# Nyström attention with a squared-ReLU MLP: the landmark sums of batches 4 to 7 go to GpSimd, and the plan around them is laid out anew

## The chip, the core and the metric

The kernel runs on one core of a Trainium2 chip. The metric is device time in microseconds (us) of one execution; a time is the median of several executions. The engines have their own instruction queues, each run in order: PE (TensorE matmul), ACT (ScalarE), DVE (VectorE), POOL (GpSimd) and SP (SyncE, which here only issues the stores). The loads are issued from POOL's queue, between POOL's computing instructions.

## The reference, cut to what matters

```python
def _attn_ref(q, k, v):                      # 8 batches, 8 heads, 576 rows, 64 columns, fp32
    q_lm = q.reshape(B, H, 32, 18, D).mean(axis=3)     # 32 landmarks, each a mean of 18 rows
    k_lm = k.reshape(B, H, 32, 18, D).mean(axis=3)
    A, Bm, C = sm(q, k_lm), sm(q_lm, k_lm), sm(q_lm, k)   # softmax(scale * a @ b^T)
    Z = Bm^T / (norm1(Bm) * norminf(Bm) + 1e-06)
    for _ in range(6):
        Z = 2 * Z - Z @ Bm @ Z
    return A @ Z @ C @ v

def _moe_ref(x, w_in, w_out):                # x: 4608 tokens x 512, d_ff = 2048
    r = np.maximum(x @ w_in, 0.0)
    return (r * r) @ w_out
```

## The kernel before, in words

Each of the 8 batches has an attention part and an MLP part. Nothing of the attention's result is written out: (Z C v) is multiplied into `w_in` first, which gives a matrix WP per batch, and the MLP's first matmul takes A (transposed) against WP.

**The operations and their names.** The program makes a list of small operations, named by kind, batch and part. For batch b, with the profile's line of each:

- loads on POOL's queue, cast to bf16 on the way: `ldk`, `ldq` (L462), `ldv` (L471), `win` (L481), `wout` (L492). X has 3 buffers, LM 2.
- `lm` sums the 18 rows of every landmark, as matmuls against an identity on PE. Batches 0 and 1 (`FLAT_LM`) take 18 matmuls of 128x128 for each half of the heads (L521, 128 columns each). Batches 2 to 7 take 36 matmuls on 64x64 quarters of the array with 256 columns (L532), which leave two partial sums in two banks: `lmc` (ACT, L552, two copies) brings one to SBUF as LS, `lme` (DVE, L555) adds the other. In batches 0 and 1 `lme` is a plain copy on ACT (L449). `lmt` transposes the result (DVE, L561).
- `T` transposes q and k by blocks (DVE, L506, four a batch).
- `B`, `Bmx` ... `Brn`, `Yi`, `Zi`: the small softmax and the start of the iteration. `N` and `U`: the six steps (PE L666 or L671, DVE L680), with `bd` (L620) which spreads an operand to a block diagonal on POOL or DVE; `Zm` (L759) does it at the end.
- `SC`, `Cmx`, `Cex`, `CT`: the softmax of C and its transpose (PE L697, DVE L708, ACT L714, DVE L719). `Crc` takes the reciprocal of C's row sums, after putting them in the order of the next matmul's output: one copy of 128x2 (L726), four of 32x1 (L729), a reciprocal (L731), all on DVE. `CV` (PE L740, 72 matmuls), `CVe` (DVE L749), `ZC` (PE L766), `ZCe` (L449), `W` (PE L786, 8 matmuls each), `We` (L449 on ACT or L453 on DVE, 128x1024).
- `SA`, `At`, `Amx`, `Asb`, `Aex`, `Asu`, `Arc`, `Aml`, `Ab`: the softmax of A in two parts of 10 and 8 of the 18 segments (PE L808; DVE L833, L836, L840; ACT L842; DVE L844, L847, L850, L853).
- `F` (PE L879): A against WP, 16 pieces of hidden columns a batch, in batches 0 and 1 two parts (320 and 256 columns), so 32 pieces. `R` (ReLU, ACT L896 or DVE L898) and `Q` (square, ACT L905 or DVE L907) bring each piece to G in SBUF. A piece holds one of 4 banks kept for F until its R is done (two banks, when it has 576 columns).
- `O` (PE L925): four groups of four matmuls of 512 columns for each of the 36 output tiles; `Oe` copies out, `St` stores.
- `fill` (L1036): matmuls on ones without use, which fill PE's gaps at the start.

**What sets the order.** A planner (`Plan.schedule`) runs the list against costs that are written in the program (`v_`, `ap_`, `a_`, `g_`, `pe`), chooses an engine where an operation allows several, and gives banks of PSUM. Where several operations are ready, the one with the longest chain behind it (`tail`) goes first; `URGE` shifts this by kind and batch, and `PATIENCE` holds an operation back from one engine in favour of another. An operation with `port` waits, in the plan, until the port of POOL and DVE is free. The instructions are then issued to each engine in the plan's order. On the chip only data, banks and buffers hold an instruction back, and each engine keeps its order.

In the order of before, PE reaches the first `F` with `W0.0 W0.1 fill F0.0`, and then runs F and O pieces with the attention of later batches between them. `F1.0`, the first MLP piece of batch 1, comes behind 14 groups of O; in the changed program it comes behind 10.

Of the kernel before, what the change touches and what calls it, by code (L numbers as in the profile page):

```python
# [8 lines left out]
P = 128  # L9
AF = mybir.ActivationFunctionType  # L10
ALU = mybir.AluOpType
AX = mybir.AxisListType
BF16 = mybir.dt.bfloat16
F32 = mybir.dt.float32
# [5 lines left out]
D = 64  # L20
M = 32
SEG = S // M
# [30 lines left out]
class Plan:  # L53
# [2 lines left out]
    SW_LANES = 8  # L56


    BLOCK, FETCH, FETCH_LOADED, PROLOG = 256, 3.8, 6.2, 80

    SWITCH = 0.092

# [2 lines left out]

    def op(self, name, engs, emit, R=(), W=(), alloc=(), nbytes=0, queue=None, after=(), bias=0.0,
           crit=False, port=(), mode="full", ni=8):
        o = Op()
        o.crit, o.port, o.mode, o.ni = crit, port, mode, ni
        o.name, o.engs, o.emit = name, engs, emit  # L70
        o.deps, o.succ, o.tail, o.seq = set(), [], 0.0, len(self.ops)
        o.alloc, o.nbytes, o.queue, o.bias = list(alloc), nbytes, queue, bias
        o.eng = o.start = o.end = None
        o.uses = [x for x in {id(x): x for x in [*R, *W] if isinstance(x, Bank)}.values()]
        for x in o.uses:
            x.users += 1
        for x in R:
            if x in self.last_w:
                o.deps.add(self.last_w[x])
        for x in W:  # L80
            if x in self.last_w:
                o.deps.add(self.last_w[x])
            o.deps.update(self.readers.get(x, ()))
        for x in R:
            self.readers.setdefault(x, []).append(o)
        for x in W:
            self.last_w[x] = o
            self.readers[x] = []
        o.deps.update(after)
        o.deps.discard(o)  # L90
        self.ops.append(o)
        return o
# [183 lines left out]
    def fillers(self, until, width, emit):  # L276

        busy = sorted((o.start, o.start + o.engs["PE"] + 0.1) for o in self.ops if o.eng == "PE")
        found, at = [], 1.5
        for a, b in busy:  # L280
            if a > until:
                break
            n = min(int((a - 0.2 - at) / width), 8 if at < 6 else 2)
            if n > 0:
                for j in range(8):
                    if all(h[1] >= a or h[2] <= at - 0.1 for h in self.history if h[0] == j):
                        found.append((a - 0.2 - n * width, j, n))
                        break
            at = max(at, b)
        for at, j, n in found:  # L290
            o = Op()
            o.name, o.eng, o.start, o.seq = f"fill{at:.0f}", "PE", at, -1
            o.engs, o.end, o.tail, o.mode = {"PE": n * width}, at + n * width, 0.0, "full"
            o.emit = lambda e, j=j, n=n: emit(j, n)
            self.ops.append(o)
# [11 lines left out]
def ap_(n):  # L307
    return 0.046 + 0.00083 * n


def v_(n, fast=False):
    return 0.07 + (0.00052 if fast else 0.00104) * n


def g_(n):
    return 0.15 + 0.0022 * n
# [28 lines left out]
def pe(n, k=1):  # L345
    return k * max(n * 0.000424, 0.027)
# [3 lines left out]
def kernel(  # L350
# [9 lines left out]
    nc = tc.nc  # L360
# [3 lines left out]
    def mk(name, shape, dt):  # L364
        return sb.tile(shape, dt, name=name, tag=name)
# [3 lines left out]
    def bank(x, i=0):  # L369
        return ps[:, x.at + i, :]  # L370
# [4 lines left out]
    def pair(x, n):  # L375
        return ps[:, x.at:x.at + 2, 0:n]
# [2 lines left out]
    V = [mk(f"V{i}", [P, 2, SEG, D], BF16) for i in range(3)]  # L379
    TT = [mk(f"TT{i}", [P, 2, 2, SEG, M, 2], BF16) for i in range(2)]  # L380
    LM = [mk(f"LM{i}", [P, 2, 2, D], BF16) for i in range(2)]
    LS = [mk(f"LS{i}", [P, 256], F32) for i in range(2)]
    LT = [mk(f"LT{i}", [P, 2, 2, M, 2], BF16) for i in range(2)]
    SAt = [mk(f"SA{u}", [P, 2, n, M], F32) for u, n in enumerate(A_LEN)]
    Anorm = [mk(f"An{u}", [P, 2, n // 2, M, 2], BF16) for u, n in enumerate(A_LEN)]
# [24 lines left out]
    ident = mk("ident", [P, P], BF16)  # L410
# [6 lines left out]
    op = pl.op  # L417
# [8 lines left out]
       R=["identf"], W=["ident"])  # L426
# [10 lines left out]
    def c_blk(e):  # L437
# [3 lines left out]
       R=["onesf"], W=["warm"])  # L441
# [4 lines left out]
    def copy(e, o, i, scale=None):  # L446
        if e == "ACT":
            if scale is None:
                nc.scalar.copy(o, i)  # L449
            else:  # L450
                nc.scalar.activation(o, i, AF.Copy, scale=scale)
        elif scale is None:
            eng(e).tensor_copy(o, i)  # L453
        else:
            eng(e).tensor_scalar(out=o, in0=i, scalar1=scale, scalar2=None, op0=ALU.mult)
# [40 lines left out]
    def attention(b):  # L496
        x, tt, lm, lt = X[b % 3], TT[b % 2], LM[b % 2], LT[b % 2]
        kx = lambda t, r: ("X", b % 3, t, r)
        kt = lambda t, r: ("TT", b % 2, t, r)
        i2 = b % 2  # L500
        quad = lambda i: slice(32 * i, 32 * i + 32)
# [8 lines left out]

        flat = b in FLAT_LM
        rss = ((0,), (1,)) if b in SPLIT_LM else ((0, 1),)
        pls = [Bank(1, "att") for _ in rss] if flat else [Bank(2, "att")]
        pl_ = pls[0]

        def lmx(e, rs):
            if flat:
                for s in range(SEG):  # L520
                    nc.tensor.matmul(  # L521
                        bank(pls[rs[0]])[:, 0:128 * len(rs)].rearrange("p (t x) -> p t x", t=2)
                        .rearrange("p t (r d) -> p t r d", d=D),
                        lhsT=ident[:], rhs=x[:, :, rs[0]:rs[-1] + 1, s, :],
                        start=(s == 0), stop=(s == SEG - 1))
                return
            o = pair(pl_, 256).rearrange("p j (t r d) -> p j t r d", t=2, r=2)
            for s in range(9):
                for j in range(2):
                    for h in range(2):  # L530
                        i, z = slice(64 * h, 64 * h + 64), 64 * (h ^ j)
                        nc.tensor.matmul(o[z:z + 64, j], lhsT=ident[i, i],  # L532
                                         rhs=x[i, :, :, 9 * j + s, :],
                                         start=(s == 0), stop=(s == 8))

        for rs in rss:
            op(f"lm{b}.{rs[0]}", {"PE": pe(128 * len(rs), 18 if flat else 9) + 0.03},
               lambda e, rs=rs: lmx(e, rs), R=["ident", *[kx(t, r) for t in range(2) for r in rs]],
               W=[pls[rs[0]]], alloc=[pls[rs[0]]],
               mode="full" if flat else "64x64", ni=36 if flat else 72)  # L540
        if flat:
            for rs in rss:
                op(f"lme{b}.{rs[0]}", {"ACT": ap_(128 * len(rs)), "DVE": v_(128 * len(rs))},
                   lambda e, rs=rs: copy(
                       e, lm[:, :, rs[0]:rs[-1] + 1],
                       bank(pls[rs[0]])[:, 0:128 * len(rs)].rearrange("p (t r d) -> p t r d",
                                                                      t=2, d=D)),
                   R=[pls[rs[0]]], W=[("LM", i2, r) for r in rs])
        else:
            def lmc(e):  # L550
                for h in range(2):
                    nc.scalar.copy(LS[i2][64 * h:64 * h + 64],  # L552
                                   bank(pl_, 1)[64 - 64 * h:128 - 64 * h, 0:256])
            op(f"lmc{b}", {"ACT": 0.77}, lmc, R=[pl_], W=[("LS", i2)])
            op(f"lme{b}", {"DVE": v_(256)}, lambda e: nc.vector.tensor_tensor(  # L555
                lm[:].rearrange("p t r d -> p (t r d)"), bank(pl_)[:, 0:256], LS[i2][:], ALU.add),
               R=[pl_, ("LS", i2)], W=[("LM", i2, 0), ("LM", i2, 1)])
        kLT = lambda r: ("LT", i2, r)
        for rs in rss:
            sl = slice(rs[0], rs[-1] + 1)  # L560
# [162 lines left out]


        def crc(e):
            nc.vector.tensor_copy(s_[:, 16:18], s_[:, 14:16])  # L726
            for p in range(4):
                z = 2 * (p // 2) + 1 - p % 2
                nc.vector.tensor_copy(s_[quad(z), 16 + p % 2:17 + p % 2],  # L729
                                      s_[quad(p), 15 - p % 2:16 - p % 2])  # L730
            nc.vector.reciprocal(s_[:, 16:18], s_[:, 16:18])  # L731
        op(f"Crc{b}", {"DVE": 0.45}, crc, R=[kb("csm0"), kb("csm1")], W=[kb("crc")])
        pV = Bank(2, "att")


# [313 lines left out]
        "Bnm", "Bad", "Brn", "BBT", "Zi", "Yi", "N", "U", "ZC", "ZCe", "W", "We"}  # L1049
CRIT_B = (0,)  # L1050
SQ_ACT = tuple(range(B))
SPLIT_LM = (0,1)
SPLIT_A = (0,)
FLAT_LM = (0,1)
SA_LATE = (0,)
W_CH = 1

PATIENCE = {"DVE": 0.4}

STRETCH = (1.2, 2.5)  # L1060

URGE = {
    "Aml0": 17, "Aml2": -18, "Amx0": -26.9, "Asb1": -13.2, "At0": 4.5, "BBT2": -20.7,
    "BBT6": -17, "Blo2": -5.9, "Bmb0": 1.6, "CT0": -10.2, "CV3": -4.9, "CVe0": 66.5,
    "Cex1": 35.8, "F0": -27.3, "N1": 27.6, "N3": 46.9, "O0": 29.4, "O1": -1.9, "Q0": 22.2,
    "R0": 162.5, "R1": 8.2, "SA1": 67.9, "SA2": 61.8, "T1": -15.2, "We0": 60.5, "Yi0": 23.4,
    "Zi1": -21.7, "lm1": -67.5, "lm2": -65.6, "lmc3": 11.7
}
POOL_A = ()
POOL_M = ()  # L1070

PARTS = (0,1)
WEAVE = {0: 0.0, 1: 0.5}
LIMITS = {"att": 6, "h": 4, "o": 4}

# [33 lines left out]
```

## Time and profile before

| What | us |
|---|---|
| median of 3 runs (272.32 to 272.54) | 272.36 |
| the profiled execution, whole | 273.66 |
| the profiled execution, span from first to last instruction | 272.0 |
| PE busy in the span | 256.7 |
| ACT busy | 209.4 |
| DVE busy | 180.5 |
| POOL busy | 50.5 |

The span is that of the profiled execution; 1.7 us lie around it. The instructions of one engine overlap a little: their rows give the time from start to end of each, and the next may start some 0.1 us ahead of the end of one that it doesn't depend on. A matmul's row of 0.38 us for 512 columns contains the time until its result has landed; in a stream, matmuls of 512 columns start every 0.215 us. So sums over an engine's queue are made from start to start. The granted TensorE clock is 1.00 throughout.

### The profile page before, as it was taken

How to read it: one execution, taken by the hardware profiler on the slowest of the kernel's cores; microseconds unless marked ns; L12 is line 12 of the kernel's file. 1: busy time of each engine (PE TensorE's matmuls, PEld its weight loads, DVE VectorE, ACT ScalarE, POOL GpSimd, SP SyncE). 2: the span in 40 equal slices, each digit the busy share in tenths (PEclk: the TensorE clock that was granted, in tenths of full speed). 3: DMA queues.
4: the chain of work that ended last, by engine and by line, in shares of the span. 5: the costliest groups of instructions: out<-in, count | busy, mean ns of one | idle time of the engine just before them, and what ended most of it. 6: DMA issues, size and time to landing. Idle time of an engine off the chain costs nothing.

```text
span 272.0 us, 7590 instructions
## 1 busy us (share of the span) xinstructions
PE 256.7 (94%) x3070; PEld 143.8 (53%) x3070; DVE 180.5 (66%) x533; ACT 209.4 (77%) x422; POOL 50.5 (19%) x93
## 2 busy tenths in 40 slices
PE   5868899999999999999999999999999999999993
PEld 1636355455565666465545564555546564555452
DVE  2489999878999789849952898249864898000000
ACT  2033898899999979998799799998829989999110
POOL 8443823634240022000400010000000000000000
PEclk9999999999999999999999999999999999999999
DMA  6999999999996192611542101221031110311333
GB/s 104 202 210 209 204 204 212 232 220 214 242 226 129 41 156 64 126 39 41 85 83 61 46 14 40 58 62 39 4 80 39 41 42 0 80 39 39 80 77 77
DMA packets 16259, 28.28 MB, mean 104 GB/s; under 512 B 2272, under 2 KB 4576, under 8 KB 16224
## 3 DMA queue, kind: packets, MB, share of 16 engines
q0 software_dynamic: 10304, 18.35, 37.5%
q1 hardware_dynamic: 5840, 9.38, 14.0%
q8 instruction: 24, 0.39, 0.6%
q14 instruction: 11, 0.09, 0.1%
q10 hardware_dynamic: 80, 0.07, 0.1%
HBM read 36.70 MB, written 9.44 MB: 170 GB/s over the span
## 4 chain that ended last, share of the span: by engine, by line
PE 51%; DVE 22%; ACT 18%; issue 6%; DMA 2%; POOL 1%; ACTq 0%; DVEq 0%; POOLq 0%
PE ps L925 28%; PE ps L879 13%; ACT RS L896 6%; ACT G L905 5%; ACT WP L449 3%; DVE TT L506 2%; DVE SA L833 2%; PE ps L786 2%; PE ps L532 2%; DMA X<-in_q_dram 2%; DVE G L907 2%; PE ps L697 2%; DVE CT L719 1%; PE ps L521 1%; DVE sm L729 1%
## 5 line engine op out<-in xcount | busy, mean ns | idle before, releaser
L925 PE MATMUL ps<-w_out,G 128*128 128x512 bf16 (+1 forms) x592 | 141.1, 373 | 0.3 <-DVE ST L680 0.3
L896 ACT ACTIVATE RS<-ps 128x576 bf16<-128x576 f32 (+2 forms) x152 | 79.5, 562 | 8.1 <-PE ps L879 5.9
L879 PE MATMUL ps<-AT,WP 128*128 128x288 bf16 (+2 forms) x512 | 80.4, 286 | 1.4 <-ACT WP L449 0.6
L925 PEld LDWEIGHTS <-G 128*128 128x128 bf16 x592 | 55.1, 98 | 49.8 <-issue 4.5
L905 ACT ACTIVATE G<-RS 128x576 bf16<-128x576 bf16 (+2 forms) x119 | 66.3, 590 | 1.5
L879 PEld LDWEIGHTS <-WP 128*128 128x128 bf16 x512 | 46.6, 97 | 28.8 <-issue 7.0
L449 ACT COPY OS<-ps 128x512 f32<-128x512 f32 (+2 forms) x34 | 19.1, 569 | 17.8 <-PE ps L925 17.8
L907 DVE TENSOR_TENSOR G<-RS 128x576 bf16<-128x576 bf16 (+2 forms) x41 | 16.3, 406 | 20.2 <-ACT RS L896 19.9
L449 ACT CAST WP<-ps 128x1024 bf16<-128x1024 f32 x27 | 26.7, 1025 | 3.3 <-PE ps L786 3.3
L506 DVE STREAM_TRANSPOSE TT<-X 128x576 uint32<-128x576 uint32 x32 | 24.0, 758 | 4.9 <-DMA X<-in_k_dram 4.4
L620 POOL TENSOR_TENSOR BD<-ST,blkb 128x256 bf16<-128x256 bf16 x10 | 6.7, 667 | 106.0 <-DVE ST L680 56.4
L708 DVE TENSOR_REDUCE sm<-ps 128x1 f32<-128x576 f32 x16 | 11.5, 750 | 10.4 <-PE ps L697 10.4
L714 ACT ACTIVATE C<-ps,sm 128x576 bf16<-128x576 f32 x16 | 14.1, 906 | 5.5 <-DVE sm L711 5.5
L680 DVE SCALAR_TENSOR_TENSOR ST<-ST,ps 128x128 bf16<-128x128 bf16 (+1 forms) x48 | 12.6, 261 | 7.2 <-PE ps L666 6.7
L453 DVE COPY OS<-ps 128x512 f32<-128x512 f32 (+1 forms) x4 | 2.3, 579 | 22.4 <-ACT OS L449 22.4
L471 POOL DMA_DIRECT2D V<-in_v_dram x24 | 12.7, 538 | 7.6 <-DMA w_in<-in_moe_w_in_dram 2.2
L833 DVE STREAM_TRANSPOSE SA<-ps 128x320 f32<-128x320 f32 (+1 forms) x32 | 12.8, 449 | 1.4 <-ACT RS L896 0.9
L786 PE MATMUL ps<-w_in,ZC 64*32 64x512 bf16 x256 | 12.1, 383 | 1.3 <-ACT ZC L449 0.7
L462 POOL DMA_DIRECT2D X<-in_k_dram x16 | 9.0, 564 | 20.6 <-PE ps L532 14.3
L842 ACT ACTIVATE SA<-SA 128x640 f32<-128x640 f32 (+1 forms) x16 | 10.2, 680 | 3.2 <-DVE SA L840 3.2
L844 DVE TENSOR_REDUCE smA<-SA 128x20 f32<-128x640 f32 (+1 forms) x16 | 11.7, 744 | 1.0 <-ACT SA L842 0.9
L850 DVE TENSOR_TENSOR An<-SA,smA 128x640 bf16<-128x640 f32 (+1 forms) x16 | 12.2, 790 | 0.0
(81 smaller groups left out, 253.2 us busy)
## 6 DMA issues: line engine op xcount, KB each, us to landing
out_dram<-OS SPq DMA_DIRECT2D x70, 128.0 KB, 2.4
X<-in_k_dram POOLq DMA_DIRECT2D x16, 288.0 KB, 10.4
X<-in_q_dram POOLq DMA_DIRECT2D x16, 288.0 KB, 9.7
V<-in_v_dram POOLq DMA_DIRECT2D x8, 288.0 KB, 9.2
w_in<-in_moe_w_in_dram POOLq DMA_DIRECT2D x8, 256.0 KB, 10.3
w_out<-in_moe_w_out_dram POOLq DMA_DIRECT2D x4, 512.0 KB, 11.0
V<-in_v_dram POOLq DMA_DIRECT2D x8, 216.0 KB, 9.4
V<-in_v_dram POOLq DMA_DIRECT2D x8, 72.0 KB, 8.8
```

The source lines that it names most:

```text
L449: nc.scalar.copy(o, i)
L471: lambda e, r=r, p0=p0, n=n, src=src: nc.gpsimd.dma_start(vv[32 * p0:32 * (p0 + n), r].rearrange("p s d -> p (s d)"), src),
L506: op(f"T{b}.{t}{r}", {"DVE": v_(576)}, lambda e, r=r: nc.vector.transpose(tt[:, t, r].rearrange("p s m e -> p (s m e)").bitcast(U32), x[:, ...
L680: nc.vector.scalar_tensor_tensor(out=o, in0=i0, scalar=2.0, in1=bank(pN)[:, 0:2 * w].rearrange("p (r w) -> p r w", r=2), op0=ALU.mult, op1 ...
L714: op(f"Cex{b}.{r}", {"ACT": a_(576) + 0.27}, lambda e, r=r, pS=pS: nc.scalar.activation(Cs[r][:].rearrange("p x u -> p u x"), pair(pS, HAL ...
L786: nc.tensor.matmul(ps[quad(p), pW.at + z, :], lhsT=ZC[i2][half, p, :], rhs=w_in[half, at_win(c, r), 512 * ch:512 * ch + 512], start=True, ...
L833: nc.vector.transpose(sa[:, z].rearrange("p s m -> p (s m)"), ps[:, pS.at + z, 0:M * n])
L879: nc.tensor.matmul(ps[:, ph.at + i, 0:w], lhsT=wp[:, r, 128 * f:128 * f + 128], rhs=at[:, r, lo + w * i:lo + w * i + w], start=(r == 0), s ...
L896: nc.scalar.activation(o, x, AF.Relu)
L905: nc.scalar.activation(o, x, AF.Square)
L907: nc.vector.tensor_tensor(o, x, x, ALU.mult)
L925: nc.tensor.matmul(bank(po)[:, 0:c1 - c0], lhsT=G[:, f, lo:lo + P], rhs=w_out[:, f, c0:c1], start=(f == 0), stop=(f == NF - 1))
```

## The change

```diff
-    BLOCK, FETCH, FETCH_LOADED, PROLOG = 256, 3.8, 6.2, 80
+    BLOCK, FETCH, FETCH_LOADED, PROLOG = 256, 3.8, 6.2, 100
...
-            n = min(int((a - 0.2 - at) / width), 8 if at < 6 else 2)
+            n = int((a - 0.2 - at) / (width if at > 6 else 2 * width))
...
+        def landmarks(rs):
+            n, sl, flat = 128 * len(rs), slice(rs[0], rs[-1] + 1), (b, rs[0]) in FLAT_LM
...
+            ls, kS = LS[i2][:, rs[0]], ("LS", i2, rs[0])
+            for h in range(2):
+                op(f"lmc{b}.{rs[0]}{h}", {"ACT": 0.17 + 0.00083 * n, "DVE": v_(n)},
+                   lambda e, h=h: copy(e, ls[64 * h:64 * h + 64, 0:n],
+                                       bank(pl_, 1)[64 - 64 * h:128 - 64 * h, 0:n]),
+                   R=[pl_], W=[(kS, h)])
...
+        if b in POOL_LM:
+            for t in (1, 0):
+                lp = LP[t]
+                k_ = lambda a, n, t=t: [("LP", t, i) for i in range(a, a + n)]
+                steps = [(a, n, x[:, t, :, a:a + n], x[:, t, :, a + 9:a + 9 + n], [kx(t, 0), kx(t, 1)])
+                         for a, n in ((0, 2), (2, 2), (4, 2), (6, 2), (8, 1))]
+                steps += [(a, n, lp[:, :, a:a + n], lp[:, :, w + a:w + a + n], k_(a, n) + k_(w + a, n))
+                          for a, n, w in ((0, 2, 4), (2, 2, 4), (0, 2, 2), (0, 1, 1))]
+                for i, (a, n, i0, i1, R) in enumerate(steps):
+                    op(f"lp{b}.{t}{i}", {"POOL": g_(128 * n)},
+                       lambda e, a=a, n=n, i0=i0, i1=i1, lp=lp: nc.gpsimd.tensor_tensor(
+                           lp[:, :, a:a + n], i0, i1, ALU.add),
+                       R=R, W=k_(a, n), port=("POOL",))
+                op(f"lp{b}.{t}9", {"POOL": g_(128)}, lambda e, t=t, lp=lp: nc.gpsimd.tensor_tensor(
+                    lm[:, t], lp[:, :, 0], lp[:, :, 8], ALU.add),
+                   R=k_(0, 1) + k_(8, 1), W=[("LM", i2, 0), ("LM", i2, 1)], port=("POOL",))
+        else:
             for rs in rss:
+                landmarks(rs)
...
-            nc.vector.tensor_copy(s_[:, 16:18], s_[:, 14:16])
             for p in range(4):
-                z = 2 * (p // 2) + 1 - p % 2
-                nc.vector.tensor_copy(s_[quad(z), 16 + p % 2:17 + p % 2],
-                                      s_[quad(p), 15 - p % 2:16 - p % 2])
+                for r in range(2):
+                    z = 2 * (p // 2) + r
+                    nc.vector.tensor_copy(s_[quad(z), 16 + p % 2:17 + p % 2],
+                                          s_[quad(p), 14 + r:15 + r])
...
-SPLIT_LM = (0,1)
+SPLIT_LM = (0,)
-FLAT_LM = (0,1)
+FLAT_LM = ((0, 0), (1, 0))
+POOL_LM = (4, 5, 6, 7)
-PATIENCE = {"DVE": 0.4}
+PATIENCE = {"DVE": 0.1}
-POOL_A = ()
+POOL_A = (0,)
```

- Batches 4 to 7: the `lm`, `lmc` and `lme` operations are gone. In their place stand 20 additions `lp` a batch on POOL, 10 for k and 10 for q: first rows 0 to 8 plus rows 9 to 17 from bf16 to fp32, then a tree in fp32; 14 of them have 256 elements a partition, 6 have 128 (two of these write LM).
- Batch 0: the first half of the heads stays as it was; the second half takes the 64x64 form with 128 columns, with two `lmc` copies and an adding `lme`. Batch 1: one sum of 18 matmuls with 256 columns for two of 128. Batches 2 and 3: as before, but the two `lmc` copies are operations of their own and may be on DVE.
- `Crc`: eight copies of 32x1 in place of one of 128x2 and four of 32x1.
- The `Asb` of batch 0 may go to POOL (`POOL_A`).
- Nearly all entries of `URGE`, `PATIENCE`, `PROLOG` and the rule for the fillers are others. With them the order on every engine is another, and so is the choice of engine: 37 of the `Q` go from ACT to DVE (27 of them with 576 columns), and so do 15 `R`, 6 `ZCe`, 3 of the `lmc` copies and one `Oe`; of the `bd` three more are on POOL, of the `Zm` three fewer.

## The prediction, made before the changed kernel was run

> **What bounds the kernel now.** First the page's busy times and slices:
>
> ```profile
> PE 256.7 (94%) x3070; PEld 143.8 (53%) x3070; DVE 180.5 (66%) x533; ACT 209.4 (77%) x422; POOL 50.5 (19%) x93
> ...
> PE   5868899999999999999999999999999999999993
> ...
> DVE  2489999878999789849952898249864898000000
> ACT  2033898899999979998799799998829989999110
> POOL 8443823634240022000400010000000000000000
> ```
>
> PE is full from the fifth slice (27 us) to the end. DVE and ACT are nearly full too from there to about 110 us; POOL is free from 80 us on. The sums by stretches say it more sharply (columns: stretch, its length, busy us with counts of PE, PEld, DVE, ACT, POOL):
>
> ```profile
> 0.00:29.70 29.70, 21.69 (x369) 12.10 (x370) 19.72 (x66) 7.93 (x19) 16.27 (x33) 1.00 1.00 184
> 29.70:56.80 27.10, 26.19 (x290) 13.90 (x291) 24.38 (x68) 24.47 (x62) 12.46 (x22) 1.00 1.16 216
> 56.80:110.00 53.20, 52.79 (x797) 31.51 (x796) 48.02 (x145) 50.88 (x127) 13.62 (x25) 1.00 0.79 156
> 110.00:170.00 60.00, 58.89 (x706) 32.90 (x698) 45.09 (x134) 52.98 (x93) 6.83 (x11) 1.00 0.28 59
> ```
>
> So from the first F (29.68 us) on, the end is PE's work in a row, plus small stalls; by start-to-start times in PE's timeline those over 0.15 us add up to 7.4 us after 36 us, none over 0.5. Whatever leaves PE after the first F is gained whole, unless DVE, second in line, then falls behind. The groups that the change touches (line, engine, operation, count | busy us, mean ns | idle before):
>
> ```profile
> L905 ACT ACTIVATE G<-RS 128x576 bf16<-128x576 bf16 x68 | 46.0, 687 | 1.5
> L907 DVE TENSOR_TENSOR G<-RS 128x576 bf16<-128x576 bf16 x28 | 12.5, 454 | 19.9 <-ACT RS L896 19.7
> L532 PE MATMUL ps<-X,ident 64*64 64x256 bf16 x216 | 6.7, 271 | 0.0
> L620 POOL TENSOR_TENSOR BD<-ST,blkb 128x256 bf16<-128x256 bf16 x10 | 6.7, 667 | 106.0 <-DVE ST L680 56.4 <-DVE sm L726 49.7
> L729 DVE COPY sm<-sm 32x1 f32<-32x1 f32 x32 | 4.6, 145 | 0.6
> ```
>
> **PE's ledger.** One `lm` of L532 takes 0.98 to 1.11 us from start to next start, 1.07 in the middle. Batches 4 to 7: 4 x 1.07 = 4.28 us gone. All count, since they lie at 93 to 190 us.
>
> **The start, walked along the new order** with durations from the rows of the same operation. The second half of batch 0's `lm` has 36 matmuls with 128 columns; a warm one with 256 columns takes 1.18, the flat form took 1.95, PE still runs at half pace there (0.43 us for a filler of 512 columns, 0.215 later): 0.96 to 1.95, I take 0.96, the columns at that pace. It waits for q's second half (landed at 10.6) and now stands ahead of `SC0.0`, which moves from 10.18 to 11.7; `Cmx0.0` (12.98) stands ahead of `lmt0.1` on DVE, so `B0` starts at 13.95, as before (13.96). Then DVE has, ahead of `U0.0`: `Crc0` (8 x 0.155 + 0.17 = 1.4), `CT0.1`, both `At`, `Amx` and `Asb0.0`. `U0.0` moves from 19.47 to 23.7. The later steps have less between them: `U0.5` ends at 27.8 (26.24 before), `ZC0` 28.15, `We0.0` 29.65 to 30.65, and `F0.0` starts at **30.75, 1.1 later**. `Asb0.1` on POOL (two pieces of 667 ns, 1.33) lies beside DVE's U steps and delays no load by more than 2 us; `wout0`, next behind, isn't needed until 37.
>
> From there ACT and DVE set the pace of F: starts every 0.33 (R of 320), 0.28 (R of 256), 0.36 and 0.31 (Q on ACT), 0.28 (Q of 320 on DVE), We 0.95. `O0.0` comes at 37.8 (37.61 before), with four more F done (1.03 us) but `CV1`, `SA1` and `SC1` (1.13 + 0.77 + 1.37) still to do: PE is 2.4 us behind. On DVE the chain `T1`, `Cmx1`, `CT1` (45.1), `Crc1`, `At1.0`, `Asb1.0` (49.0), `CVe1` (51.2), `Aml1.0`, `Ab1.0` ends at 56.25; ACT's `We1.0` at 55.25. `F1.0` starts at **56.45; before 56.84**.
>
> What is left behind F1.0: before, 272.0 - 56.84 = 215.1. Changed: four more O groups (+3.46, 0.865 each), `W1.3` (+0.34), `lm2` and `B2` already done (-1.07, -0.18), the four `lm` gone (-4.28): 213.4. Span 56.45 + 213.4 = 269.85 against 271.95: **-2.1 us**.
>
> **Can DVE keep up?** Added up along its order, a DVE op counted by its row: 53.7 us to the end of `Ab1.0`, 95.4 to `Ab2.1`, 121.0 to `Ab3.1`, 149.1 to `Ab4.1` (before: 45.3, 73.6, 107.2, 136.7). It does 1.18 us of rows in 1 us (85.3 from `Ab0.0` to `Ab3.1` in the 72 that it was busy). So `Ab2.1` ends at 56.25 + 41.7/1.18 = 91.6, `Ab3.1` 113.3, `Ab4.1` 137.1. PE reaches `F2.0`, `F3.0`, `F4.0`, which need them, at about 91.6, 119.8 and 144.8. No slack at F2.0, 6 to 8 us later. ACT gets 36 us lighter (41 Q of 576 for 68, each 687 ns there, 454 on DVE), and so do its waits. Crc: 9 instructions for 6, +0.4 us a batch on DVE, 3.4 in all, in these sums.
>
> **The price of POOL's additions.** POOL's 667 ns for 256 bf16 elements is the nearest row for one of 256; fp32 output may cost nothing more or double it, 0.67 to 1.33; I take 0.67, and 0.36 for 128: 14 x 0.67 + 6 x 0.36 = 11.5 us a batch, 46 in all, beside PE. Batch 4's stand behind k4's landing (some 66), `bt3` and V5's issues, and end at 86; `lmt4.0` waits on DVE for them at 93.5, with `T4`, the `R` and `Q` of F2 behind it. Batches 5 to 7 end near 107, 122 and 134; wanted at 108, 128 and 149. POOL's loads of batches 5 to 7 move behind the pieces by 5 to 20 us, and are wanted from 96 us on: hidden. At 1.33 batch 5's would end near 125, 17 us late, and PE some 10 us with it (282; 0.02, counted with the third rival).
>
> The real cost is that POOL and DVE hold each other. Two places in the timeline:
>
> ```profile
> 125.52 0.66 POOL L620 TENSOR_TENSOR BD<-ST,blkb 128x256 bf16<-128x256 bf16 x1 [16.49 <-DVE ST L680]
> 125.74 0.47 DVE L726 COPY sm<-sm 128x2 f32<-128x2 f32 x1
> ```
>
> ```profile
> 42.14 0.67 POOL L620 TENSOR_TENSOR BD<-ST,blkb 128x256 bf16<-128x256 bf16 x1 [2.38 <-DVE ST L680]
> 42.57 0.92 DVE L840 TENSOR_TENSOR SA<-SA,smA 128x640 f32<-128x640 f32 x1
> ```
>
> The copy takes 0.12 to 0.16 elsewhere, and ended here 0.02 us behind POOL: held 0.32. The subtraction is 0.82 elsewhere: held 0.1. Only 18 such POOL ops ran; now 46 us of them fall into 66 to 134 us, about 60% of that time. In that stretch DVE starts 49 operations with two SBUF operands (17 Q, 14 `bd`, 12 `Asb` and `Aml`, 6 others). Never held: 0; always held a whole piece: 49 x 0.67 = 33 us. I take 0.6 x 0.21 (the mean of the two rows): 6.2 us, 1.3 of it ahead of F2.0. The later 5 fit into DVE's slack; the 1.3 do not. Adding the 0.7 by which PE may be early there, and taking off 1.1 of the 1.9 us of stalls that PE had between F1.0 and F2.0 and that lie in the same wait: **+0.9**.
>
> The Trainium skill ("SBUF — State Buffer", section "Who interferes with whom") states that a VectorE instruction with two SBUF inputs and a GpSimd instruction that reads SBUF exclude each other for the whole instruction; the trace's copy, held to POOL's end, agrees, and copies of 32x1, of which the new `Crc` is made, show none (143 to 148 ns beside POOL). By this rule a hit costs what is left of a piece, 0.33 on average: 0.6 x 0.33 x 49 = 9.7 us. That result is the third rival.
>
> **Sum.** -2.1 + 0.9 = -1.2; 272.36 - 1.2 = **271.2 us**. The sum is made against the profiled span, and the difference set on the median; the profiled execution's whole, 273.66, lies 0.5% above that median. Under 0.2% (0.54 us) a measurement of this kernel doesn't tell from no change.
>
> **The rivals.**
> - *Stalls go too* (0.13; 268.3 to 270.2). ACT's 36 us less take away half of PE's 5 us of small stalls behind F1.0, and holds stay hidden: 272.36 - 2.1 - 2.5 = 267.8 at best. For it: ACT's 50.9 of 53.2 us; against: DVE is as full afterwards.
> - *No change* (0.12; 271.8 to 272.9). DVE waits for others as it did before, 2 us before F2.0.
> - *DVE, held by POOL, becomes the bound: slower* (0.25; 273 to 276). With 9.7 us of holds `Ab4.1` ends at 146.8, 2 behind PE's 144.8, and F2.0 waits 2 more; with 14 us, 6. It decides from about 4 us of holds that reach PE: 272.36 - 2.1 + 2 to 6 = 272.3 to 276.3. Against it: pieces are short and DVE may find POOL waiting for it.
> - *The start is worse than walked* (0.10; 273 to 275): `lm` of batch 0 at 1.95 and the waits for N1 and CV1 add 3 us.
> - The forecast itself (0.40): 270.2 to 271.8.
>
> Faster by over 0.2%: 0.40 + 0.13 = 0.53; within: 0.12; slower: 0.35. The range 268.3 to 276.0 leaves out little but a doubled price of the pieces.
>
> **What would show it.** In the changed profile: F0.0 near 30.8, F1.0 near 56.5; `lp` rows of 0.67; Q of 576 on DVE at 454 ns, with longer ones only beside POOL; PE idle ahead of F2.0 at most 2 us, none ahead of F3.0 and F4.0. A mean of those Q above 0.55, or PE waiting on `Ab2`, `Ab4` or `LM`, makes it wrong on the slow side; F1.0 before 55 on the fast one.

## The result and the profile after

The changed kernel takes **299.72 us** (median of 6 runs, 297.92 to 300.97); the kernel before took 272.76 us on the same chip (6 runs). The ratio is 1.098, 95% interval [1.0935, 1.1024]: **slower by 27.0 us**, far outside the forecast. The medians in this document leave out two runs that fell in a slower state of the chip, one of experiment 2 (312.60 us) and one of experiment 10 (276.94). The profiled execution has a span of 299.3 us. Busy times and slices of the page after, the lines that answer to those of before:

```profile
PE 258.6 (86%) x2939; PEld 140.4 (47%) x2939; DVE 233.9 (78%) x614; ACT 181.6 (61%) x352; POOL 101.4 (34%) x174
...
PE   4987999997996768976069999999999999999994
...
DVE  2699999999999998999967969999985698434000
...
POOL 8536435365885391969930000100000000000000
PEclk9799999999999997999659999999999999999999
```

PE is busy for 2 us more in a span 27 us longer: its row now has holes from the tenth slice to the twenty-first (67 to 157 us), and one slice is 0. DVE's row is full there. In three of these slices PE's granted clock is 0.5 to 0.7, so what it does behind a hole takes longer too. The stretches of 10 us (same columns as before; the last three are PE's granted clock, the busy share of the DMA engines and GB/s):

```profile
110.00:120.00 10.00, 7.40 (x40) 4.05 (x38) 8.62 (x15) 5.79 (x10) 3.28 (x8) 0.83 0.02 4
120.00:130.00 10.00, 9.27 (x81) 4.41 (x80) 9.80 (x21) 5.81 (x11) 10.00 (x14) 1.00 0.24 54
130.00:140.00 10.00, 7.33 (x130) 3.69 (x129) 9.23 (x25) 6.32 (x10) 6.95 (x14) 1.00 0.40 62
140.00:150.00 10.00, 1.25 (x8) 0.47 (x5) 9.97 (x3) 1.33 (x2) 10.00 (x16) 0.72 0.10 26
150.00:160.00 10.00, 7.69 (x45) 4.25 (x46) 6.44 (x13) 4.42 (x7) 2.10 (x6) 0.59 0.12 26
```

Read the row 140 to 150: DVE is busy for 9.97 us with **three** instructions, POOL for 10.00 with 16, PE for 1.25. A busy engine is not an engine at work: one DVE instruction fills the row. DVE and POOL in the timeline there (start, duration, engine, line, operation, out<-in, count):

```profile
140.54 11.71 DVE L634 TENSOR_TENSOR BD<-ST,blkb 128x256 bf16<-128x256 bf16 x1
```

```profile
139.43 1.19 POOL L566 TENSOR_TENSOR LM<-LP 128x128 bf16<-128x128 f32 x2
140.59 5.02 POOL L563 TENSOR_TENSOR LP<-X 128x256 f32<-128x256 bf16 x8
145.58 4.11 POOL L563 TENSOR_TENSOR LP<-LP 128x256 f32<-128x256 f32 x6
149.66 0.41 POOL L563 TENSOR_TENSOR LP<-X 128x128 f32<-128x128 bf16 x1
...
151.25 0.85 POOL L566 TENSOR_TENSOR LM<-LP 128x128 bf16<-128x128 f32 x2
```

`bd4.3`, a product with both operands in SBUF that takes 0.29 us alone, starts 0.05 us ahead of the 20 `lp` pieces of batch 7 and ends at 152.25, 0.15 us behind the end of the last of them. It got no turn at any of the ends between two pieces. PE waits for it:

```profile
140.23 1.03 PE L939 MATMUL ps<-w_out,G 128*128 128x512 bf16 x4
152.31 0.29 PE L680 MATMUL ps<-ST,BD 128*128 128x64 bf16 x2 [11.05 <-DVE BD L634]
152.41 2.11 PE L893 MATMUL ps<-AT,WP 128*128 128x288 bf16 x8
```

The eight matmuls of F behind the hole take 2.11 us; eight of them took 1.15 at 135 us, at full clock. So the hole costs a little more than its length.

I counted as held each DVE operation that ran beside a POOL addition or product and took at least 0.15 us more than the median of its line and shape: 22 of them, **29.0 us** above those medians; the kernel before has one, 0.3 us. (The expectations below speak of 27.5 us, from a narrower count.) Four carry most of it: `bd4.3` 11.71 us (0.29 alone), `Bml4` 3.31 (0.22), `Zi3` 2.53 (0.23), `bd4.2` 2.40 (0.29). The groups of the page after (columns as before), and its waits (engine, line, what it waited for: us in total, times, longest). The mean of `bd` on DVE is 848 ns, where it was 280 before (the third line, from the groups of before), and the longest waits of PE and of ACT, which waits for PE, are this one hold:

```profile
L563 POOL TENSOR_TENSOR LP<-X 128x256 f32<-128x256 bf16 (+1 forms) x40 | 25.8, 665 | 0.1
L634 DVE TENSOR_TENSOR BD<-ST,blkb 128x256 bf16<-128x256 bf16 x29 | 24.6, 848 | 0.4
```

```profile
L620 DVE TENSOR_TENSOR BD<-ST,blkb 128x256 bf16<-128x256 bf16 x32 | 9.0, 280 | 0.6
```

```profile
ACT RS L910 <- PE ps L893: 38.5, 33, 11.7
...
PEld L680 <- DVE BD L634: 18.2, 9, 11.5
...
PE ps L680 <- DVE BD L634: 14.8, 5, 11.1
```

### The profile page after: what moved, and what is told of

It is laid out like the page before. It is cut to its first block, busy times and chain, and to the rows that moved or that the text cites. A ratio compares the mean times of both kernels' runs of the same rounds, so it can differ in the third digit from the quotient of the medians.

```text
span 299.3 us, 7431 instructions
## 1 busy us (share of the span) xinstructions
PE 258.6 (86%) x2939; PEld 140.4 (47%) x2939; DVE 233.9 (78%) x614; ACT 181.6 (61%) x352; POOL 101.4 (34%) x174
## 4 chain that ended last, share of the span: by engine, by line
PE 47%; DVE 34%; ACT 9%; issue 5%; DMA 2%; POOL 1%; ACTq 0%; DVEq 0%; POOLq 0%
PE ps L939 26%; PE ps L893 15%; DVE BD L634 6%; ACT RS L910 3%; DVE G L921 3%; DVE SA L847 2%; DMA X<-in_q_dram 2%; DVE sm L722 2%; PE ps L800 2%; DVE smA L850 2%; DVE TT L507 2%; DVE sm L743 2%; DVE ST L694 2%; DVE RS L912 1%; ACT G L919 1%
## 5 line engine op out<-in xcount | busy, mean ns | idle before, releaser
L910 ACT ACTIVATE RS<-ps 128x576 bf16<-128x576 f32 (+2 forms) x137 | 71.9, 563 | 43.2 <-PE ps L893 38.5
L893 PE MATMUL ps<-AT,WP 128*128 128x288 bf16 (+2 forms) x512 | 82.5, 293 | 8.8 <-DVE SA L847 2.6
L921 DVE TENSOR_TENSOR G<-RS 128x576 bf16<-128x576 bf16 (+2 forms) x78 | 36.1, 467 | 21.9 <-ACT RS L910 21.6
L919 ACT ACTIVATE G<-RS 128x576 bf16<-128x576 bf16 (+2 forms) x82 | 43.9, 569 | 2.4 <-DVE RS L912 1.6
L563 POOL TENSOR_TENSOR LP<-X 128x256 f32<-128x256 bf16 (+1 forms) x40 | 25.8, 665 | 0.1
L634 DVE TENSOR_TENSOR BD<-ST,blkb 128x256 bf16<-128x256 bf16 x29 | 24.6, 848 | 0.4
L680 PE MATMUL ps<-ST,BD 128*128 128x64 bf16 (+1 forms) x84 | 9.5, 194 | 15.2 <-DVE BD L634 14.8
L563 POOL TENSOR_TENSOR LP<-LP 128x256 f32<-128x256 f32 (+1 forms) x32 | 21.4, 688 | 0.0
L680 PEld LDWEIGHTS <-BD 128*128 128x128 bf16 x84 | 6.5, 98 | 24.2 <-DVE BD L634 18.2
L912 DVE TENSOR_SCALAR RS<-ps 128x576 bf16<-128x576 f32 (+2 forms) x23 | 13.7, 604 | 2.5 <-PE ps L893 1.8
```

The source lines that it names most:

```text
L563: lambda e, a=a, n=n, i0=i0, i1=i1, lp=lp: nc.gpsimd.tensor_tensor(lp[:, :, a:a + n], i0, i1, ALU.add),
L634: bdiag = lambda e, o, i: eng(e).tensor_tensor(o.rearrange("p r (c m) -> p r c m", c=4), i.unsqueeze(2).to_broadcast([P, 2, 4, M]), blkb[: ...
L680: nc.tensor.matmul(bank(pN)[:, w * r:w * r + w], lhsT=BD[it % 2][:, r, :], rhs=av[:, lo:64], start=True, stop=True)
L893: nc.tensor.matmul(ps[:, ph.at + i, 0:w], lhsT=wp[:, r, 128 * f:128 * f + 128], rhs=at[:, r, lo + w * i:lo + w * i + w], start=(r == 0), s ...
L910: nc.scalar.activation(o, x, AF.Relu)
L912: nc.vector.tensor_scalar(out=o, in0=x, scalar1=0.0, scalar2=None, op0=ALU.max)
```

## The experiments

Theories and rivals are lettered anew from group to group of experiments; the texts quoted say what each letter means. The first four ran on one chip, with the kernel before at 273.09 us.

**1. Without the pieces.** The order of all engines stays that of the changed kernel; 72 of the 80 additions issue nothing, and the last of each chain writes LM from 2 of the 18 rows.

```diff
-   op(f"lp{b}.{t}{i}", ..., lambda e, ...: nc.gpsimd.tensor_tensor(lp[:, :, a:a + n], i0, i1, ALU.add), ...)
+   op(f"lp{b}.{t}{i}", ..., lambda e: None, ...)
```

> The changed kernel with its order of instructions kept on every engine, but 72 of the 80 additions on POOL left out; the last of each chain writes LM from two of the 18 rows, so the landmark sums of batches 4 to 7 are not those of the reference. Theory H (DVE's instructions with two SBUF operands are held by POOL's uninterrupted runs; 27.5 us of longer DVE rows in the changed profile): the time falls to that of PE's work, 299.7 - 27 to 31, that is 268 to 273, and no such DVE row is longer than its usual one by more than 0.7 us. Rival O (the new order and DVE's 37 more squares are what PE waits for): at least 285. Rival L (PE and DVE wait for late landmarks): 268 to 273 too, but then DVE's waits ahead of the transposes of LM were long in the changed profile.

Measured: **272.93 us**, ratio 1.000 [0.998, 1.002]. All of the 27 us is the pieces' doing; the other parts of the change come to nothing together. One part of the expectation was missed: a DVE row, `Zi3`, is still 1.0 us longer than usual, beside a DMA issue and a `bd` on POOL. PE is full again in the stretch that was empty:

```profile
140.00:150.00 10.00, 10.00 (x108) 5.10 (x106) 7.47 (x24) 9.12 (x14) 0.00 (x0) 1.00 0.19 44
```

**2. A gap behind each piece.** A POOL memset of one column behind every one of the 72 L563 pieces.

```diff
-   nc.gpsimd.tensor_tensor(lp[:, :, a:a + n], i0, i1, ALU.add)
+   nc.gpsimd.tensor_tensor(lp[:, :, a:a + n], i0, i1, ALU.add); nc.gpsimd.memset(gap[:], 0.0)
```

> The changed kernel, same order, all additions, and behind each of them a POOL memset of one element a partition, which reads nothing from SBUF. Theory H in the form that DVE gets no turn between two POOL instructions that follow without a gap: with a turn after each piece a hold is at most one piece (0.7 us), and the time falls to 270 to 277. If a memset gives no turn, it stays at 297 to 305. Rival O: no change, 297 to 303.

Measured: **306.11 us**, ratio 1.120 [1.113, 1.128], slower still. The holds add up to 34.1 us. The longest is now another kind of operation, a contiguous product of Q (0.45 us alone), held beside 26 pieces and 22 memsets (timeline):

```profile
143.45 14.90 DVE L922 TENSOR_TENSOR G<-RS 128x576 bf16<-128x576 bf16 x1
```

So another POOL instruction in between, one that reads nothing, is no gap. The Trainium skill ("SBUF — State Buffer", section "Who interferes with whom") says that such a DVE operation is in conflict only with a GpSimd instruction that reads SBUF, not with one that only writes; by it a memset would let DVE in. The first bench below agrees for a run of memsets alone (0.25 us); between two additions the measurement decides, and there it does not.

**3. Landmarks of batches 4 to 7 back on PE** (`POOL_LM = ()`; the planner made a new order, so this isn't one part alone).

> The changed kernel with the landmark sums of batches 4 to 7 back on PE, all else as changed; the planner lays the order out again. Theory H: no long holds, PE has 4.3 us of sums more than in the run without the pieces: 268 to 276. Rival O (the rest of the change costs): 285 or more.

Measured: 279.11 us, ratio 1.022 [1.019, 1.026], with no hold. That lies above theory H's range and below rival O's. Its PE is busy for 261.1 us, against 254.1 in experiment 1; four `lm` are 4.3 of these 7.0. The rest was not traced to a cause: the offsets of the changed kernel were made for another set of operations.

**4. First bench: what does one hold cost?** A kernel that computes nothing of the reference: POOL runs of n additions, one DVE operation laid beside each.

```python
nc.gpsimd.tensor_tensor(L[:, i, 0:w], go[:, 0:w], X[:, i, 0:w], ALU.add)          # n times
nc.vector.tensor_tensor(pr[:, 0:256], a1[:, 0:256], a2[:, 0:256], ALU.mult)       # some 0.2 us into the first
```

> No part of the reference is computed: a table of cases, each a run of POOL instructions that starts at a DVE write, and beside it one DVE probe some 0.8 us later. Theory H: a DVE product of two SBUF tensors (0.29 us alone) lasts to the end of POOL's run: 1, 2, 4, 8, 16 pieces of 0.67 us give about 0.3, 0.9, 2.2, 4.9 and 10 us; a probe with one SBUF operand (with PSUM, or a reduction, or a copy of 32x1) keeps its time. Rival P (a hold ends with the piece, as the prediction priced it): at most 0.9 us whatever the length of the run. With a memset behind each piece: H lets it in after one piece.

Measured: the product, 0.25 us alone, took 0.60 to 0.62 us beside 1, 2, 4, 8 and 16 pieces alike, 0.37 beside pieces of 128 and 1.10 beside pieces of 512: to the end of one piece, as the prediction had priced it (rival P), and not to the end of the run (theory H). Three in a row had turns in between (0.61, 0.75, 0.75). Beside one-operand copies it took 0.33, beside memsets 0.25; a DVE operation with one operand in SBUF wasn't held, apart from the fp32 copy 128x2 (0.49). That contradicted the kernel, where pieces of this size held for 20 in a row. The bench in the timeline, DVE's product and the pieces beside it:

```profile
26.46 2.59 POOL L61 TENSOR_TENSOR L<-go,X 128x256 f32<-128x256 bf16 x4 [0.59 <-DVE go L104]
26.66 0.61 DVE L76 TENSOR_TENSOR pr<-a,a 128x256 bf16<-128x256 bf16 x1
```

**5. Second bench: the real patterns.** The pieces of one batch with their strides and order, the real forms of `bd`, `Bml`, `Zi` and Q, and contiguous ones, at several moments of a piece.

```diff
+   ad(LP[t][:, :, a:a + n], X[:, t, :, a:a + n], X[:, t, :, a + 9:a + 9 + n], ALU.add)   # 8 times, then the tree
+   tt(BD..., ST[...].to_broadcast([P, 2, 4, M]), blkb[...].to_broadcast([P, 2, 4, M]), ALU.mult)
```

> Nothing of the reference is computed; runs of GpSimd additions of 256 elements are laid beside one VectorE operation with both operands in SBUF. The runs are either contiguous (as in the first bench), or with the strided patterns and the order of one batch's landmark pieces (20 of them in a row); the VectorE operations are contiguous bf16 and fp32 products, Q's form (576), and the three that were held longest in the changed kernel: the block-diagonal copy (0.29 us alone, held 11.71), Bml (0.22, held 3.31) and Zi (0.23, held 2.53), each arriving at up to three different moments of a piece. Theory A (it is the VectorE operation's form, a broadcast operand, that gets no turn): the block-diagonal copy, Bml and Zi last 5 to 13 us beside both kinds of run, the contiguous ones at most 0.8. Theory C (it is the pieces' strided form): every VectorE operation lasts several us beside the strided runs, and at most 0.8 beside the contiguous. Theory T (it is the moment of arrival): the same form is held long at one moment and for one piece at another. Theory W (it takes something else of the whole kernel, its other engines or transfers): none lasts over 1.1 us here.

Measured: beside contiguous pieces, and beside X pieces alone, every form had its turn (0.29 to 0.69). Beside the full batches, laid end to end, from the second on, **every** form was held, the contiguous ones too: 7.9 to 8.4 us, once 19.59, at each of the moments; the hold ended as a rule at the first 128-element piece, and beside the next few there were turns. In the timeline:

```profile
116.45 8.08 DVE L85 TENSOR_TENSOR BD<-ST,blkb 128x256 bf16<-128x256 bf16 x1
...
120.26 4.12 POOL L68 TENSOR_TENSOR LP<-LP 128x256 f32<-128x256 f32 x6
124.34 0.48 POOL L70 TENSOR_TENSOR LP<-X 128x128 f32<-128x128 bf16 x1
```

Theories A and T fell. C fell too, since the same X pieces let DVE in when nothing but X pieces ran. So did W: holds of 8 us come without the kernel's other engines and transfers. The Trainium skill ("SBUF — State Buffer", section "Who interferes with whom") says that the order of issue and not the form decides who blocks; the runs agree on the form.

**6. Third bench: the kind of piece.** Thirteen kinds of runs (bf16, fp32, in place, strided, mixed, the full batch), each started by a wait of POOL on DVE, one `Bml` every 2 us.

> Nothing of the reference is computed. In the bench before, no form of VectorE operation and no moment of arrival decided: beside the full order of a batch's pieces even a contiguous product was held for 8 us, until the first addition of 128 elements, while beside runs of the first eight pieces alone (X, bf16 in, fp32 out) each got a turn after one piece. Here one VectorE operation (Bml's form, 0.14 us of lock) is laid four times beside each of 13 kinds of GpSimd runs, each started afresh: X pieces alone, contiguous bf16, LP<-LP pieces alone (fp32 in, in place), the same into another tile, contiguous fp32 in three forms (two tiles, in place, one bf16 operand), 128-element fp32, LP<-LP ahead of X and behind X, the two taking turns, and the full order. Theory D (fp32 operands on both sides make GpSimd keep the port): every run with two fp32 operands holds the operation to its end (5 us or more), bf16 runs for at most 0.6. Theory H2 (it is what ran before: X pieces behind fp32 pieces hold, X pieces ahead of them don't): lx and fx hold through the X pieces, xl lets the operation pass in its first half. Theory S (it is being in step: runs of equal pieces let VectorE in at each end, runs of mixed pieces don't): x, c, l, f2, f3 all give turns, only the mixed runs hold.

Measured: no hold over 0.68 us in 104 cases, the full batch included. The kind of piece doesn't decide (D and H2 fell, and the mixed runs that S asked for gave turns). What was left: here each run started afresh, and DVE asked often.

**7. Fourth bench: what ran before.** First pieces of fifteen kinds, then eight X pieces, DVE asks only in those.

> Nothing of the reference is computed. In the last bench no run that was started afresh held a VectorE operation beyond the current piece, the full order of a batch included; the bench before held it for 8 us where GpSimd went from one full batch to the next without a stop. Here each case starts afresh, runs some first pieces (none, eight X, eight contiguous, six LP<-LP, the additions of 128 elements, the last ones into LM, the same into fp32, small ones, a full batch, three full batches), then eight X pieces; VectorE's operations come only in the X pieces. Theory H2 (something that ran before brings the eight GpSimd cores out of step, so that no common gap is left between pieces): with none, x8 and c8 the operations last at most 0.7 us; with the first pieces that do it (the full batch and one or more of its parts) the first of them lasts to the end of the X pieces, 4 to 5 us. Theory L (only long unbroken work does it): only the three full batches hold. Theory F (neither): none lasts over 0.7 us.

Measured: turns at 0.23 to 0.50 us behind up to 10 first pieces; behind a full batch (20 pieces) or three, 4.84 and 4.61 us, to the end of the X pieces. F fell. L had named only the three batches; if 20 pieces are long enough, L fits, and so does H2, if it takes the whole mixture.

**8. Fifth bench: length or mixture.** The same with 16 to 32 equal pieces ahead, with parts of the batch, and with breaks.

```diff
+   "x16": [xs] * 2, "c24": [8 contiguous] * 3, "lnm": [tree, 128s, LM], "stop": [batch, POOL waits for DVE once],
+   "mid": [first half, one DVE operation, second half], "copy": [batch, POOL copy], "set": [batch, POOL memset]
```

> Nothing of the reference is computed. In the last bench only the cases with a full batch ahead (20 pieces, 13 us without a stop) held VectorE, to the end of the eight X pieces (4.84 us); cases with at most 10 pieces ahead didn't. Theory L (the length of the unbroken run decides, whatever the pieces): 16, 24 and 32 equal pieces ahead hold as well, from some length on. Theory K (the mixture decides): equal pieces never hold, and the one part that does it shows in the cases that leave a part out (X and LP<-LP; those and the 128s; without X; without LP<-LP; and so on). Beside both: a full batch and then a stop of GpSimd (it waits for VectorE once) brings the turns back, 0.5 us; a VectorE operation that had its turn in the middle of the batch shortens the unbroken run from 20 to 12 pieces: by L no hold, by K a hold. A copy or a memset on GpSimd behind the batch tells whether a one-operand instruction is a break (turn, 0.5 us) or not (4 us or more).

Measured: in this bench **length decides**, whatever the pieces. Every operation that came 8.0 us (17 POOL instructions) or more after POOL's last stop, with no turn in between, was held to the end of the run, equal pieces as well; every one at 7.3 us (15) or less had its turn. After `stop` the turn was back (0.47 and 0.23 us); `copy` and `set` broke nothing (4.84 and 4.61). After a turn in the middle of a run, one operation had its turn 6.12 us later, another, at 6.36 us, was held. A turn and a hold in the timeline, the latter in the case `xnm`, the shortest that held:

```profile
303.89 3.21 POOL L63 TENSOR_TENSOR LP<-X 128x256 f32<-128x256 bf16 x5
...
304.17 0.47 DVE L147 TENSOR_TENSOR Bf<-Bl,s__75 128x64 f32<-128x64 f32 x1
```

```profile
363.83 5.04 POOL L63 TENSOR_TENSOR LP<-X 128x256 f32<-128x256 bf16 x8
...
364.12 4.84 DVE L147 TENSOR_TENSOR Bf<-Bl,s__75 128x64 f32<-128x64 f32 x1
```

**9 and 10. Stops in the kernel itself.** Ahead of each of the 80 pieces DVE writes one column at that place of its own order, and POOL must wait for it. POOL has *more* to do by this. Experiment 10 has the waits without the pieces (landmarks from two rows of 18).

```diff
+   nc.vector.memset(tick[:, g, 0:1], 0.0)
+   nc.gpsimd.memset(tick[:, g, 0:2], 0.0)
    nc.gpsimd.tensor_tensor(lp[:, :, a:a + n], i0, i1, ALU.add)
```

> The changed kernel in its own order, with a wait of GpSimd on VectorE ahead of each of the 80 pieces: VectorE writes one column of a small tile at that place of its order (some 0.06 us each, 5 us in all), GpSimd reads it into its queue by writing over it (0.05 to 0.2 us), then does the piece. The benches say that a run of GpSimd that starts afresh gives VectorE its turn after one piece, and one unbroken for 8 us or more none to its end. Theory L (unbroken runs are the cost): no VectorE operation is held by more than the pieces whose waits it has already passed, the 11.7 us hold breaks up into holds of 1 to 2 us, the sum of the holds falls from 27.5 us to some 8 to 12, and the time to 280 to 286 us. Theory G (what decides in the kernel is something other than unbroken length, as another engine's traffic): holds of several pieces stay, 295 us or more. Landmarks that come too late would show as B of batches 5 to 7 waiting, not as holds.

> The same with the 72 pieces left out (landmarks of batches 4 to 7 from two rows of 18), so only the waits and the small writes are left: what they cost by themselves. At 0.06 us each on a VectorE that is not the bound, all theories expect 272.5 to 275 us; what e6 has above this run is the pieces' own cost with the waits in place.

Measured, before at 273.16 us: with the waits **275.95 us**, ratio 1.013 [1.009, 1.016], 24 us faster than the changed kernel; the waits alone 274.85, ratio 1.006 [1.003, 1.009]. The pieces, with their stops, cost **some 1 us** (the runs of experiment 10 differ by 3.6 us among themselves). Theory L had forecast holds of 8 to 12 us and 280 to 286 us; the stops did better than that. In the groups of experiment 9, forms apart, Q (L926) has a mean of 467 ns against 454 before, and `bd` (L639) 360 against 280 before and 848 in the changed kernel; its waits show POOL waiting for the tick:

```profile
L926 DVE TENSOR_TENSOR G<-RS 128x576 bf16<-128x576 bf16 x55 | 25.6, 467 | 20.7 <-ACT RS L915 20.6
...
L639 DVE TENSOR_TENSOR BD<-ST,blkb 128x256 bf16<-128x256 bf16 x29 | 10.4, 360 | 0.4
...
L565 DVE MEMSET tick<- 128x1 f32 x72 | 4.1, 59 | 0.0
```

```profile
POOL tick L566 <- DVE tick L565: 13.2, 19, 2.0
```

DVE waits no longer for POOL's whole run; POOL waits for DVE, 13.2 us in 19 stops, which costs the kernel no more than the 1 us above. A held DVE instruction keeps its own next tick back, so POOL can run on only over pieces whose ticks lie ahead of that instruction.

**11 and 12. Fewer stops.** Waits at 16 of the 80 pieces; waits at the 20 pieces of batch 7 alone.

```diff
+   if g % 5 == 0:     # experiment 11
+   if g >= 60:        # experiment 12
```

> The kernel with the waits of GpSimd on VectorE, but only at the first X piece and the first LP<-LP piece of each half of a batch: 16 waits in place of 80. Theory L (a hold lasts until GpSimd next stops): holds of up to 4 to 10 pieces come back beside the stretches without a wait, the time lies between, 278 to 290 us; if it is as good as with 80 waits (274 to 276 us), a few waits are enough to keep the runs short. Theory G (something other than the waits made e6 fast, as a later start of the pieces): 275 us, with no hold over two pieces even in stretches of five and more pieces.

> The waits at the 20 pieces of batch 7 alone. In the changed kernel one copy was held 11.71 us beside them, and on PE, which waits for it, the step from one output block to the next grew by 11.2 us. If that one hold is worth its length, the time falls from 299.7 by 9 to 12 us, to 288 to 291; if PE has other late things behind it, by less than 5; if the holds beside batches 4 to 6 move or grow, it can be anything above.

Measured, before at 272.69 us: 279.74 us (1.026 [1.024, 1.029]) and 287.97 us (1.058 [1.054, 1.063]). Experiment 12 takes away the hold of 11.71 us and gains 11.75 us; the holds beside batches 4 to 6 come again almost to the hundredth (2.53, 3.32, 2.40). All kernels in one table (holds counted as above, from one profile each; the longest is that of the operations held):

| kernel | holds | their sum, us | longest, us | time, us |
|---|---|---|---|---|
| 2, memset behind each piece | 22 | 34.1 | 14.90 | 306.11 |
| changed kernel | 22 | 29.0 | 11.71 | 299.72 |
| 12, stops at batch 7 | 28 | 20.0 | 3.32 | 287.97 |
| 11, 16 stops | 25 | 13.0 | 2.11 | 279.74 |
| 9, 80 stops | 19 | 7.4 | 1.31 | 275.95 |
| 10, stops without pieces | 3 | 0.7 | 0.68 | 274.85 |
| 1, no pieces | 6 | 2.5 | 1.23 | 272.93 |

The time follows the sum of the holds: from experiment 9 to experiment 2 the holds grow by 26.7 us and the time by 30.2. It is not one for one at each step; from experiment 9 to 11 the holds grow by 5.6 us and the time by 3.8. No version here beats the kernel before: even with the landmarks of batches 4 to 7 left out, the rest only equals it.

## Why the prediction was wrong

**The step that failed is the price of a hold:** "a hit costs what is left of a piece", taken as 0.21 us from two rows of the kernel before, 6.2 us in all. Those rows could not show more: behind the first of these POOL operations POOL stood idle for 5.8 us, behind the second came one DMA issue, and nowhere in the kernel before do more than two of POOL's additions or products follow each other without a pause. 46 us of pieces in long rows were a new state, and the price was carried over from the old one. Shown: in a row without a stop the hold may go on past 4 (`Zi3`), 7 (`Bml4`) and 21 (`bd4.3`) ends of pieces, 29.0 us in 22 holds. Where stops keep the rows short (experiment 9), the forecast's size comes back: 19 holds, 7.4 us, and some 1 us on the time (275.95 - 274.85) where the prediction had +0.9. That these agree so well is partly luck: the forecast had 29 holds of 0.21 us, the profile has 19 of 0.39. What was said ahead of the prediction, that only data, banks and buffers hold an instruction back, leaves out this fourth cause, another engine's instructions.

**Two smaller slips in the same term.** 46 us of pieces in the 68 from 66 to 134 us are 0.68 of the time, not 0.6; with that the holds come to 7.0 us. And the copy of 128x2 has one operand in SBUF, so it is no instance of the rule for two operands that it was said to agree with. Such copies are held all the same (0.49 us in the first bench; the longest hold of experiment 9, 1.31 us, is one), and the count of 49 operations left them out.

**The third rival** had the sign, and the mechanism but for what ends a hold: DVE, held by POOL, becomes the bound. Its price came from the same rule, 9.7 us (14 at the outside), so it ended at 276 where 299.7 was measured; and the range ended with it. "Always held a whole piece: 33 us" was written down as the upper end and left out of the range. It would have been near the 29.0 us counted, but by luck: what happened was few holds over many pieces, not 49 holds of one.

**The start** was forecast 1.2 to 1.4 us late: F0.0 30.75 (measured 29.46), O0.0 37.8 (36.44), `F1.0` 56.45 (55.23; before 56.84). The order of events was right.

**PE's ledger** from F1.0 on, 213.4 us. Experiment 1, which has the order without the pieces, gives 270.9 - 55.5 = 215.4. The `lm` are gone as reckoned (1.11 us for each one that is left), but the small stalls over 0.15 us after 36 us grew: taken from start to start, with 0.215 us for 512 columns, they add up to 7.7 us before and 8.8 in experiment 1. That is half of the 2.0 us; the other half is not traced. So the "-2.1" did not show in the time, and without holds the result is the second rival's, no change. ACT, which was to be 36 us lighter, was 28.7 lighter there (180.7 busy against 209.4).

**DVE's pace** held up to F2.0: `Ab2.1` ends at 92.98 in experiment 1 (forecast 91.6), with `F2.0` at 92.71 right beside it, so "no slack at F2.0" was right. Then it fell behind: `Ab3.1` 116.8 (113.3), `Ab4.1` 145.5 (137.1), just ahead of `F4.0` at 146.2. The slack of 6 to 8 us that was to swallow the later holds was 5 us and then 1.

**The pieces** themselves: 0.63 us from start to start and 0.67 each (forecast 0.67), those of 128 0.41 to 0.45 (0.36). The landmarks came in time: `lmt5.0` at 121.4, `lmt6.0` at 163.9 and `lmt7.0` at 188.3, behind sums done at 120.9, 140.6 and 152.1. That rival part is out.

**What would show it:** of the signs on the slow side, PE waiting on `Ab2` came, with 1.6 us ahead of `F2.0`. `Ab4` and `LM` did not: `F4.0` follows an O without a wait. The wait that counted, PE on `bd` (14.8 us), was not among the signs. The mean of the Q of 576 on DVE, 493 ns, stayed under the 0.55 that I had set; the four longest holds lay on other lines.

**Still open** is what in POOL and DVE decides the turn. The bench's border (7.3 to 8.0 us since POOL's last stop) is not the kernel's: there `Zi3` was held 0.7 us into a row of POOL, `bd4.3` 5.2 us into one, DMA issues included; and in the second bench, in a row of POOL that had gone on for 68 us, a hold came 2.4 us after a turn. That parts of POOL fall out of step, as one expectation has it, is a guess that no run here tests. What is shown is that a stop, in which POOL really waits, brings the turns back in the fifth bench (4.84 us without, 0.47 with), and that 80 of them take the holds of the kernel from 29.0 to 7.4 us. Whether in the kernel the stop itself gives the turn, or only the end of the row, since POOL cannot pass a tick that DVE still owes, these runs do not tell apart.

## What to carry to other kernels

A price for contention that is taken from lone instructions says nothing about rows of them: ask how long the other engine will run without a wait, and take the whole of that row as the upper bound of one hold. If POOL is to do a long job beside a DVE that matters, let it wait for DVE ahead of each piece; 80 such waits cost some 2 us here (274.85 against 272.93) and saved 24, while 16, one for five pieces, saved 20. And look at the count beside the busy time: three instructions in 10 us is not work.

## What the hardware showed that was not expected

- One DVE product with two SBUF operands lasted up to 14.90 us (experiment 2) and 19.59 us (second bench) beside POOL additions of 0.41 to 0.72 us each; alone it takes 0.45 and 0.25.
- With no turn since POOL's last stop, the fifth bench gives DVE its turn after one piece up to 7.3 us behind that stop, and none from 8.0 us on; a memset or a copy of POOL is not a stop, a wait is. In the kernel holds begin earlier.
- PE's granted clock, 1.00 from 120 to 140 us of the changed kernel, was 0.72 in the stretch where PE was busy for 1.25 of 10 us, and 0.59 in the next, where eight matmuls of F took 2.11 us in place of 1.15.
